# Attention and two gated layers on one core: where the first scores, the sums, the filler units, X's copies and the column loads stand

## The chip, the cores and the metric

One core of one Trainium2 chip. The metric is the device time of one execution in microseconds, measured on the chip. All times below come from the timed runs or from one profiled execution. The engines are named as the profile names them: PE (TensorE), ACT (ScalarE), DVE (VectorE), POOL (GpSimd), and SP (SyncE, which issues most DMAs).

## The reference, cut to what matters

The program is an attention with capped scores, then a gated layer that mixes along the sequence, then a gated convolution layer. All is float32; batch 2, 12 heads, sequence 448, head size 64, model width 768, inner width 1024.

```
scores = scale * q @ k.T;  scores = cap * tanh(scores / cap)
attn = softmax(scores);    x = attn @ v, heads side by side     # 2 x 448 x 768
h = gelu(x @ w_in);        u, v = halves of h
v_n = layer norm of v (with g_ln);  v_s = w_sg @ v_n + b_sg
y = x + (u * v_s) @ w_out
h2 = relu(y @ w2_in);      conv = three taps along the sequence (conv_w)
out = (h2 * sigmoid(conv)) @ w2_out
```

## The kernel before

Everything is computed in split form: a float32 value is kept as a high and a low part, and one product is three matmuls (`mm3`, L108 to L111).

**Attention** (`attention`, L273) works on 12 pairs of heads. A loop over half pairs R (L592) writes the program; two half pairs make a pair, N = R // 2. For a half pair, `scores` (L383) puts scores into the tile `sc` (four PSUM banks, one buffer), `soft` runs tanh on ACT from PSUM into `raw` (L394), `expo` runs exp in place (L403). In the first half pair (R = 0) the scores come in two groups of two banks, each with its own tanh and exp; all later half pairs have one tanh and one exp. The sum over the two 128-key groups, `sm`, is added on DVE (L449).

The products with v go into the tile `pv`, which is called `sums` in the code (three banks, L381): `value` (L458) multiplies the exponentials with v, the rest of `values` (L479) multiplies them with ones, which gives the softmax sums. Pairs use two overlapping ranges of the tile, so the value products of a pair wait until ACT has copied the last pair's to E (`copy`, L521). `LAGS` says by how many half pairs `values` runs behind `scores`; for the first half pair the value products come in R = 1 right behind its scores (L611).

`norm` (L505) takes two pairs of heads at a time: the sums go through DRAM to be reciprocals spread over partitions (POOL's DMAs, L523, L545, L551), DVE multiplies E with them (L558), and `split` writes the high part of X on ACT (L105) and the low part on DVE (L106). The last pair takes a way over PE (`norm_pe`, L567). Steps are put off by `later(k, fn)`, k ticks on; there are two ticks in each R.

`idle` matmuls (L440, the table `IDLE`) multiply zeros in the bank `mo`: four behind the first scores group, two behind the scores of R = 1, nine behind those of R = 3.

**Filler.** The table `FILL` puts the first four units of the next layer (18 matmuls each, `mmw`) into the attention: unit 0 in thirds at R = 15, 19 and 23, in the bank `mo`; units 1, 2 and 3 at R = 24, 25 and 26 in the banks 1 to 3 of one tile `fi`, which takes the place of `sc` (L633). `u_done` runs their gelu: a square on ACT (L221), a product on DVE (L224), a tanh on ACT (L225), a product u on DVE (L228).

**Loads.** SP issues the DMAs in the order of the program: q, k and v of coming pairs, and a piece of `w_in` at each R of `WIN`. A piece lands in one of four buffers (`f64`) and is converted by `decode_half` (L134): a head on ACT or DVE (L149, L151), three steps on DVE. `columns` (L269, called at R = 6) loads g_ln and the small conv_w and converts the latter on ACT and DVE (L149, L154, L158, L163).

**The rest** (`rest`, L712) runs on PE without a hole in before: units of u (`u_unit`) and of v (`v_unit`, L746), which take seven banks of a new pool and, every fourth, the bank `mo`, then the mix along the sequence, the out projection and the convolution layer. A scheduler orders each engine's instructions from the program's order and from its own estimate, but `ordered` (L374) keeps the attention's matmuls in the order written, and `pin` holds ACT's and DVE's marked steps behind each other.

Of the kernel before, what the change touches and what calls it, by code (L numbers as in the profile page):

```python
# [9 lines left out]
F32 = mybir.dt.float32  # L10
# [9 lines left out]
P = 128  # L20
# [12 lines left out]
LAGS = (1, 2, 3)  # L33
# [6 lines left out]

WARM = 18

IDLE = {0: (0, 4), 1: (3, 2), 3: (3, 9)}

WIN = (3, 5, 7, 9, 12, 15, 17, 19, 21, 22, 23, 24)
WOS = (0, 1, 4, 7, 7, 10, 11, 15)
# [5 lines left out]
def stages(  # L52
# [23 lines left out]
    def pin(last):  # L76
        return tc.issue_after(last[0].ins) if last[0] is not None else ExitStack()
# [11 lines left out]
    def later(k, fn):  # L89
        due.setdefault(now[0] + k, []).append(fn)  # L90
# [177 lines left out]

    def columns(pool):  # L269
        sync(gbc, g_ln.partition_broadcast(P))  # L270
        decode(cw[:, 0], cw[:, 1], conv_w, pool, 4 if bounded else 3)

    def attention(att, psa):  # L273

# [105 lines left out]
        late, sm0 = [], [None]  # L380
        sums = psa.tile([P, 3 * 512], F32, tag="pv", name="pv", bufs=1)  # L381

        def scores(N, half, ahead={}):  # L383

            R = 2 * N + half
            q, K = Qt[N], Kt[N % 2]
            ps = psa.tile([P, 4, 512], F32, tag="sc", name="sc", bufs=1)
            raw = raws[N, half] = att.tile([P, 4, S], F32, tag="raw", name="raw", bufs=3)

            sc = {"scale": qscale} if N == 0 else {}  # L390

            def soft(x, ps):
                with pin(lasta):
                    lasta[0] = A.activation(x, ps, AF.Tanh, **sc)  # L394
                if N == 1 and half:
                    with pin(lasta):
                        late.pop()()
                if half or N:
                    expo(x)

            def expo(x):
                with pin(lasta):
                    lasta[0] = A.activation(x, x, AF.Exp, scale=creg)  # L403

            if half:
                ps = ps.rearrange("p (h a) c -> p h (a c)", h=2)[:, :, : 3 * 288]
                ps = ps.rearrange("p h (i c) -> p h i c", i=3)[:, :, :, :HS]
                raw = raws[N, half] = raw[:, :3].rearrange("p t s -> p (t s)").rearrange(
                    "p (h i c) -> p h i c", h=2, i=3
                )  # L410

            for g in range(2 * half, 2 * half + 2):
                if g in ahead:
                    ahead[g]()
                c = slice(g * P, (g + 1) * P)
                if g < 3:

                    for i, (j, l) in enumerate(((0, 0), (0, 1), (1, 0))):
                        for h in range(2):
                            r = slice(h * D, (h + 1) * D)  # L420
                            out, x = ps[:, g * 2 + h, :S] if g < 2 else ps[:, h, :2], q[r, l]
                            if g == 2:
                                x = x.rearrange("p (i c) -> p i c", i=2)
                            ordered(out, lhsT=K[r, j, c], rhs=x, start=i == 0, stop=i == 2)
                else:

                    qr, _ = qraw.pop(N)
                    for h in range(2):
                        r = slice(h * D, (h + 1) * D)
                        for i in range(2):  # L430
                            ordered(
                                ps[i * D : (i + 1) * D, h, 2], lhsT=klast[N % 2][r],
                                rhs=qr[r, i * HS : (i + 1) * HS], start=True, stop=True,
                            )
                if N == 0 and g < 2:
                    soft(raw[:, 2 * g : 2 * g + 2], ps[:, 2 * g : 2 * g + 2, :S])
                    if g:
                        expo(raw[:, 0:2])
                        expo(raw[:, 2:4])
                if R in IDLE and g == IDLE[R][0]:  # L440
                    for _ in range(IDLE[R][1]):
                        ordered(idle, lhsT=wz[:, :P], rhs=wz, start=True, stop=True)
            if half:
                soft(raw, ps)
            elif N:
                soft(raw, ps[:, :, :S])
            if half == 0:
                held[N] = att.tile([P, 2, S], F32, tag="sm", name="sm", bufs=2)
                sm = V.tensor_tensor(out=held[N], in0=raw[:, 0:2], in1=raw[:, 2:4], op=ALU.add)  # L449
                if N == 0:  # L450
                    sm0[0] = sm
# [53 lines left out]
        def norm(N, both):  # L505
            b, p = divmod(N, NPAIR)
            if N >= B * NPAIR - NFAST:
                return norm_pe(N, both)

            j = N % 2  # L510
            last = N == B * NPAIR - NFAST - 1
            m = 1 if last else 2
            if j == 0:
                pairs[:] = (
                    att.tile([P, 2 * (S + HS)], F32, tag="E", name="E", bufs=3),
                    att.tile([P, 14], F32, tag="ss", name="ss", bufs=2)[:, : 7 * m],
                )
            e, ss = pairs

            def copy():  # L520
                lasta[0] = A.activation(e[:, j * (S + HS) : (j + 1) * (S + HS)], both, AF.Copy)  # L521
                u = j * (2 * S + HS)
                G.dma_start(ss[j * P // m : (j + 1) * P // m], e[::32, u : u + HS])  # L523

            if N:
                copy()
            else:
                late.append(copy)
            if j == 0 and not last:
                return  # L530

            rb = att.tile([P, 2, S], F32, tag="rb", name="rb", bufs=2)
            eb = e[:, HS : HS + m * S].rearrange("p (j c) -> p j c", j=m)
            rb = rb[:, :m]

            ds = []


            def s1():
                with pin(lastv):  # L540
                    V.tensor_scalar(out=ss, in0=ss, scalar1=guard, scalar2=None, op0=ALU.add)
                V.reciprocal(out=ss, in_=ss)
                ds.append(dr.tile([m, 2, 2, HS], F32, tag=f"d{m}", name="d"))
                d = ds[0]
                G.dma_start(d.rearrange("j h f (p c) -> (j h f p) c", c=7 * m), ss)  # L545

            def s1b():
                (d,) = ds
                for h in range(2):
                    for i in range(m):  # L550
                        G.dma_start(  # L551
                            rb[h * D : (h + 1) * D, i].rearrange("p (f c) -> p f c", f=2),
                            d[i, h].partition_broadcast(D),
                        )

            def s2():
                with pin(lastv):
                    V.tensor_tensor(out=eb, in0=eb, in1=rb, op=ALU.mult)  # L558
                with pin(lasta):
                    lastv[0] = split(eb, X[:, 0, p - j : p + 1, b], X[:, 1, p - j : p + 1, b], "a")  # L560

            k = 5 if N < 8 else 4
            later(k, s1)
            later(k + 1, s1b)
            later(14 if N < 8 else 13, s2)

        def norm_pe(N, both):  # L567

# [22 lines left out]
        done = 0  # L591
        for R in range(2 * NN + LAGS[1] + 1):  # L592
            N, half = divmod(R, 2)
            if R == 6:
                columns(att)
            if R == 4:
                load_vlast(3, NN)
# [4 lines left out]
            if R < 2 * NN:  # L602
                if half == 0 and N + 2 < NN:
                    load(N + 2)
                if half == 0 and N + 1 < NN:
                    load_v(N + 1)
                if R == 1:

                    start_values(0)
                    scores(N, half)  # L610
                    value(0, 0)  # L611
                    value(0, 1)
                    values(0, 0, True)
                    done += 1
                else:
                    scores(N, half)
                if half == 0 and N + 1 < NN:
                    with pin(sm0) if N == 1 else ExitStack():
                        prep_q(N + 1)
                        prep_k(N + 1)  # L620
            if R in FILL:

                i, k0, k1 = FILL[R]
                if k0 == 0:
                    if i == 1:
                        free = psa.tile([P, 4, 512], F32, tag="sc", name="fi", bufs=1)
                    fill[i] = free[:, i, :S] if i else psm.tile([P, 512], F32, tag="mo", name="mo")[:, :S]
                for k in range(k0, k1):
                    mmw(fill[i], 0, i, k, ordered)
                if k1 == NK:  # L630
                    u_done(0, i, fill[i])
            tick()
            if done < 2 * NN and R - done >= LAGS[R >= LAGS[2]]:  # L633
                values(*divmod(done, 2))
                done += 1
            tick()
# [414 lines left out]
```

## Time and profile before

| what | value |
|---|---|
| median of 3 runs | 333.09 us (332.92 to 335.06) |
| the profiled execution | 333.06 us |
| its span, first to last instruction | 331.3 us |
| mean granted clock of PE | 0.996 |
| busy: PE, DVE, ACT, POOL | 317.9, 239.0, 222.9, 36.9 us |

The span is shorter than the execution's time by what lies around it. A share of busy time is a mean over stages with different limits; where PE is almost always busy, its few waits and the work that computes nothing are what a change can win. In the rows below, a timeline row gives start and duration in microseconds, the engine, the line, the operation, the tile written and the tiles read, the sizes, how many such instructions follow each other, and in brackets how long the engine stood idle ahead of it and what ended that.

### The profile page before, as it was taken

How to read it: one execution, taken by the hardware profiler on the slowest of the kernel's cores; microseconds unless marked ns; L12 is line 12 of the kernel's file. 1: busy time of each engine (PE TensorE's matmuls, PEld its weight loads, DVE VectorE, ACT ScalarE, POOL GpSimd, SP SyncE). 2: the span in 40 equal slices, each digit the busy share in tenths (PEclk: the TensorE clock that was granted, in tenths of full speed). 3: DMA queues.
4: the chain of work that ended last, by engine and by line, in shares of the span. 5: the costliest groups of instructions: out<-in, count | busy, mean ns of one | idle time of the engine just before them, and what ended most of it. 6: DMA issues, size and time to landing. Idle time of an engine off the chain costs nothing.

```text
span 331.3 us, 6291 instructions
## 1 busy us (share of the span) xinstructions
PE 317.9 (96%) x2391; PEld 263.5 (80%) x2391; DVE 239.0 (72%) x470; ACT 222.9 (67%) x356; POOL 36.9 (11%) x73
## 2 busy tenths in 40 slices
PE   8899999999999989999999999999999999999992
PEld 6566666566667768988899999999999999999991
DVE  4456876487467589999998798996868999990000
ACT  3799899998993257676855565545677989883110
POOL 4000134030332211112111000000000000000000
PEclk9999999999999999999999999999999999999998
DMA  5498664745732132322403690001292123013210
GB/s 141 126 202 245 209 206 126 198 152 152 241 99 54 57 123 70 91 65 70 130 6 122 195 353 8 2 0 63 64 345 102 32 65 95 0 54 118 83 59 34
DMA packets 22063, 37.75 MB, mean 114 GB/s; under 512 B 7320, under 2 KB 14376, under 8 KB 22024
## 3 DMA queue, kind: packets, MB, share of 16 engines
q1 hardware_dynamic: 20152, 34.41, 33.1%
q0 software_dynamic: 1632, 2.61, 2.9%
q8 instruction: 21, 0.34, 0.4%
q10 hardware_dynamic: 240, 0.23, 0.3%
q14 instruction: 18, 0.15, 0.1%
HBM read 34.40 MB, written 2.79 MB: 112 GB/s over the span
## 4 chain that ended last, share of the span: by engine, by line
PE 77%; ACT 10%; DMA 5%; DVE 3%; SPq 2%; issue 1%; DVEq 0%; ACTq 0%
PE mo L109 18%; PE mo L110 18%; PE mo L111 18%; PE pv L377 6%; ACT raw L394 4%; PE fi L377 3%; PE sc L377 3%; ACT raw L403 3%; PE mo L756 3%; PE mo L757 3%; PE mo L758 3%; SPq L83 2%; DMA kr<-in_kT_dram 2%; DMA f<-in_w_in_dram 2%; DMA qr<-in_qT_dram 1%; PE mo L377 1%
## 5 line engine op out<-in xcount | busy, mean ns | idle before, releaser
L111 PE MATMUL mo<-X,WI 128*128 128x448 f32 x120 | 43.8, 365 | 0.0
L110 PE MATMUL mo<-X,WI 128*128 128x448 f32 x120 | 43.8, 365 | 0.0
L109 PE MATMUL mo<-X,WI 128*128 128x448 f32 x120 | 43.2, 366 | 0.0
L403 ACT ACTIVATE raw<-raw 128x1344 f32<-128x1344 f32 (+2 forms) x25 | 36.4, 1460 | 0.6
L377 PE MATMUL pv<-raw,V 128*32 128x224 f32 x576 | 32.9, 358 | 2.1 <-ACT E L521 2.1
L110 PE MATMUL mo<-HG,W 128*128 128x448 f32 x96 | 34.7, 365 | 0.0
L111 PE MATMUL mo<-HG,W 128*128 128x448 f32 x96 | 34.7, 365 | 0.0
L394 ACT ACTIVATE raw<-sc 128x1792 f32<-128x1792 f32 (+1 forms) x22 | 32.4, 1472 | 3.3 <-PE sc L377 3.2
L109 PE MATMUL mo<-HG,W 128*128 128x448 f32 x96 | 33.3, 365 | 0.0
L179 ACT ACTIVATE f<-f 128x256 f32<-128x256 f32 (+2 forms) x44 | 22.8, 517 | 14.9 <-DMA f<-in_w_in_dram 7.9
L377 PE MATMUL sc<-Q,K 64*128 64x448 f32 x216 | 28.8, 387 | 1.6 <-ACT raw L394 1.1
L377 PEld LDWEIGHTS pv<-raw,V 128*32 128x32 f32 x576 | 18.9, 109 | 13.7 <-issue 4.9
L377 PEld LDWEIGHTS sc<-Q,K 64*128 64x128 f32 x216 | 18.4, 184 | 11.9 <-ACT raw L394 6.5
L189 DVE SCALAR_TENSOR_TENSOR f<-f 128x256 uint32<-128x256 uint32 (+2 forms) x44 | 22.4, 518 | 6.9 <-ACT f L182 6.7
L109 PEld LDWEIGHTS mo<-X,WI 128*128 128x128 f32 x120 | 22.5, 188 | 2.2 <-ACT g L225 0.4
L111 PEld LDWEIGHTS mo<-X,WI 128*128 128x128 f32 x120 | 22.5, 188 | 1.9
L110 PEld LDWEIGHTS mo<-X,WI 128*128 128x128 f32 x120 | 22.5, 188 | 1.9
L182 ACT ACTIVATE f<-f 128x256 uint32<-128x256 uint32 (+2 forms) x44 | 22.6, 514 | 0.0
L192 DVE SCALAR_TENSOR_TENSOR f<-f 128x256 uint32<-128x256 uint32 (+2 forms) x44 | 22.5, 517 | 0.2
L936 ACT ACTIVATE o<-mo 128x448 f32<-128x448 f32 x12 | 6.3, 544 | 23.0 <-PE mo L111 19.9
L449 DVE TENSOR_TENSOR sm<-raw 128x896 f32<-128x896 f32 x12 | 13.1, 1090 | 11.0 <-ACT raw L403 10.8
L109 PEld LDWEIGHTS mo<-HG,W 128*128 128x128 f32 x96 | 18.0, 188 | 1.5
(151 smaller groups left out, 700.3 us busy)
## 6 DMA issues: line engine op xcount, KB each, us to landing
f<-in_w_in_dram SPq DMA_DIRECT2D x12, 512.0 KB, 3.9
f<-in_w_out_dram SPq DMA_DIRECT2D x24, 256.0 KB, 5.0
f<-in_w_in_dram SPq DMA_DIRECT2D x12, 511.8 KB, 4.7
f<-in_w_out_dram SPq DMA_DIRECT2D x8, 384.0 KB, 3.2
qr<-in_qT_dram SPq DMA_DIRECT2D x24, 112.0 KB, 3.2
out_dram<-o SPq DMA_DIRECT2D x12, 224.0 KB, 1.9
rb<-d POOLq DMA_DIRECT2D x22, 112.0 KB, 3.5
V<-in_vL_dram SPq DMA_DIRECT2D x12, 192.0 KB, 2.6
```

What stands on the lines that cost most here:

```text
L109: matmul(ps, lhsT=whi, rhs=xhi, start=start, stop=False)
L110: matmul(ps, lhsT=whi, rhs=xlo, start=False, stop=False)
L111: matmul(ps, lhsT=wlo, rhs=xhi, start=False, stop=stop)
L179: A.activation(f(h), f(h), AF.Copy, scale=2.0**-112)
L182: A.activation(l, l, AF.Copy, scale=0.93 * 2.0**-29)
L189: V.scalar_tensor_tensor(out=l, in0=h, scalar=3, in1=l, op0=ALU.logical_shift_left, op1=ALU.bitwise_or)
L192: V.scalar_tensor_tensor(out=l, in0=h, scalar=0x80000000, in1=l, op0=ALU.bitwise_and, op1=ALU.bitwise_or)
L377: lastm[0] = T.matmul(*args, **kw)
L394: lasta[0] = A.activation(x, ps, AF.Tanh, **sc)
L403: lasta[0] = A.activation(x, x, AF.Exp, scale=creg)
L449: sm = V.tensor_tensor(out=held[N], in0=raw[:, 0:2], in1=raw[:, 2:4], op=ALU.add)
L756: T.matmul(ps, lhsT=xs(0, k), rhs=WI[1][:, 0, k], start=k == 0, stop=False)
```

## The change

Five parts, all in the attention:
1. The first scores group (R = 0, g = 0) goes into the accumulators' tile (`sums`, seen as three banks) and its tanh reads from there. `IDLE` becomes four matmuls behind the second group, none at R = 1, five at R = 3.
2. The sums of the first half pair are multiplied behind the scores of the second pair (R = 2), no longer ahead of them; `R > 1` keeps `values` from running earlier.
3. X of a pair of pairs is split in two halves: one at the old tick, one two ticks later (one tick for late pairs).
4. Filler units 2 and 3 use the one bank `mo` in turn; only unit 1 stays in a tile in the place of `sc`.
5. `columns` is called at R = 23, ahead of that R's weight piece, and its conversion steps come 5, 6 and 7 ticks behind.

```diff
-IDLE = {0: (0, 4), 1: (3, 2), 3: (3, 9)}
+IDLE = {0: (1, 4), 3: (3, 5)}
...
-        decode(cw[:, 0], cw[:, 1], conv_w, pool, 4 if bounded else 3)
+        decode(cw[:, 0], cw[:, 1], conv_w, pool, *((4, (5, 6, 7)) if bounded else (3,)))
...
-        def scores(N, half, ahead={}):
+        def scores(N, half):
...
-                if g in ahead:
-                    ahead[g]()
+                to = ps
+                if R == 0 and g == 0:
+                    to = sums.rearrange("p (t c) -> p t c", t=3)
...
-                            out, x = ps[:, g * 2 + h, :S] if g < 2 else ps[:, h, :2], q[r, l]
+                            out, x = to[:, g * 2 + h, :S] if g < 2 else ps[:, h, :2], q[r, l]
...
-                    soft(raw[:, 2 * g : 2 * g + 2], ps[:, 2 * g : 2 * g + 2, :S])
+                    soft(raw[:, 2 * g : 2 * g + 2], to[:, 2 * g : 2 * g + 2, :S])
...
                     V.tensor_tensor(out=eb, in0=eb, in1=rb, op=ALU.mult)
+                part(0)
+
+            def part(i):
                 with pin(lasta):
-                    lastv[0] = split(eb, X[:, 0, p - j : p + 1, b], X[:, 1, p - j : p + 1, b], "a")
+                    lastv[0] = split(eb[:, i], X[:, 0, p - j + i, b], X[:, 1, p - j + i, b], "a")
...
             later(14 if N < 8 else 13, s2)
+            if j:
+                later(16 if N < 8 else 14, lambda: part(1))
...
-            if R == 6:
+            if R == 23:
                 columns(att)
...
+                else:
+                    scores(N, half)
+                if R == 2:
                     values(0, 0, True)
                     done += 1
-                else:
-                    scores(N, half)
...
-                    fill[i] = free[:, i, :S] if i else psm.tile([P, 512], F32, tag="mo", name="mo")[:, :S]
+                    fill[i] = free[:, i, :S] if i == 1 else psm.tile([P, 512], F32, tag="mo", name="mo")[:, :S]
...
-            if done < 2 * NN and R - done >= LAGS[R >= LAGS[2]]:
+            if R > 1 and done < 2 * NN and R - done >= LAGS[R >= LAGS[2]]:
```

The first order shown is PE's, at the start of the program, as the difference from before to after: `wps` is warm-up, K_87 belongs to the first pair and K_88 to the second, `sm` is the summed exponentials of the first half pair.

```order
 L351 MATMUL wps<-wz 128x448 x18
+L377 MATMUL pv<-Q,K_87 128x448 x6
 L377 MATMUL sc<-Q,K_87 128x448 x6
 L377 MATMUL idle<-wz 128x448 x4
-L377 MATMUL sc<-Q,K_87 128x448 x6
 L377 MATMUL sc<-Q,K_87 128x2x224 x6
 L377 MATMUL sc<-qr,kl_91 64x224 x4
-L377 MATMUL idle<-wz 128x448 x2
 L377 MATMUL pv<-raw,V 32x224 x16
+L377 MATMUL sc<-Q,K_88 128x448 x12
 L377 MATMUL pv<-sm,ones_148 32x224 x4
-L377 MATMUL sc<-Q,K_88 128x448 x12
```

The first group now writes `pv`, the idles stand behind both groups, two idles are gone, and the second pair's twelve scores matmuls stand ahead of the four sums matmuls.

The second is PE's again, at the end of the attention, around the last filler unit: the `ones` rows end the last pair's sums, the eighteen of `fi` or `mo` are unit 3, `E,sel` is the last pair's normaliser.

```order
 L377 MATMUL pv<-raw,ones_146 32x224
 L377 MATMUL pv<-raw,ones_147 32x224
-L109 MATMUL mo<-X,WI_76 128x448
-L110 MATMUL mo<-X,WI_76 128x448
-L111 MATMUL mo<-X,WI_76 128x448
-L109 MATMUL mo<-X,WI_76 128x448
-L110 MATMUL mo<-X,WI_76 128x448
-L111 MATMUL mo<-X,WI_76 128x448
-L377 MATMUL fi<-X,WI_76 128x448 x18
+L377 MATMUL mo<-X,WI_76 128x448 x18
 L377 MATMUL pv<-E,sel 64x224 x4
```

The six matmuls of a later unit that stood ahead of unit 3 have gone from there, and unit 3 now writes the bank `mo`.

The third is ACT's, in the middle of the attention, where X is copied and a weight piece (`hd`) is converted. Before:

```order
L403 ACTIVATE raw<-raw 128x1792
L105 ACTIVATE X<-E 128x2x448
L394 ACTIVATE raw<-sc 128x1344
L403 ACTIVATE raw<-raw 128x1344
L521 ACTIVATE E<-pv 128x672
L149 ACTIVATE hd_140<-f_878 128x512
L394 ACTIVATE raw<-sc 128x1792
```

And after:

```order
L403 ACTIVATE raw<-raw 128x1792
L105 ACTIVATE X<-E 128x448
L394 ACTIVATE raw<-sc 128x1344
L403 ACTIVATE raw<-raw 128x1344
L522 ACTIVATE E<-pv 128x672
L105 ACTIVATE X<-E 128x448
L149 ACTIVATE hd_141<-f_867 128x512
L394 ACTIVATE raw<-sc 128x1792
```

The copy of two heads' X became two copies, the second behind the copy E and straight ahead of the piece's conversion and the next tanh.

## Rows read from the trace of the kernel before

**Rows 1.** The page, busy time of each engine, share of the span, instructions.

```profile
PE 317.9 (96%) x2391; PEld 263.5 (80%) x2391; DVE 239.0 (72%) x470; ACT 222.9 (67%) x356; POOL 36.9 (11%) x73
```

**Rows 2.** What PE waited for: total us, times, longest.

```profile
PE pv L377 <- ACT E L521: 2.1, 4, 0.6
PE mo L756 <- DVE u L228: 1.6, 1, 1.6
...
PE sc L377 <- ACT raw L394: 1.1, 1, 1.1
PE fi L377 <- DVE u L228: 0.5, 1, 0.5
```

**Rows 3.** Stretch, length, busy us of PE, PEld, DVE, ACT, POOL, clock, DMA, GB/s.

```profile
10.00:11.00 1.00, 0.16 (x2) 0.16 (x4) 0.00 (x0) 1.00 (x2) 0.00 (x0) 1.00 0.59 120
...
140.00:150.00 10.00, 10.00 (x48) 8.72 (x47) 10.00 (x23) 7.55 (x15) 1.00 (x1) 1.00 0.25 79
```

**Rows 4.** Timeline of the start, PE and ACT, 7.8 to 22 us.

```profile
7.80 1.01 ACT L394 ACTIVATE raw<-sc,one 128x896 f32<-128x896 f32 x1 [1.46 <-PE sc L377]
...
9.78 1.01 ACT L394 ACTIVATE raw<-sc,one 128x896 f32<-128x896 f32 x1 [0.97 <-PE sc L377]
...
10.69 1.78 ACT L403 ACTIVATE raw<-raw 128x896 f32<-128x896 f32 x2
...
10.84 0.88 PE L377 MATMUL sc<-Q,K 64*128 64x448 f32 x6 [1.10 <-ACT raw L394]
...
12.19 0.67 PE L377 MATMUL idle<-wz 128*128 128x448 f32 x2
12.37 1.37 ACT L394 ACTIVATE raw<-sc,one 128x1344 f32<-128x1344 f32 x1
...
12.79 1.76 PE L377 MATMUL pv<-raw,V 128*32 128x224 f32 x32
...
14.33 0.60 PE L377 MATMUL pv<-sm,ones 128*32 128x224 f32 x8
...
14.86 1.49 PE L377 MATMUL sc<-Q,K 64*128 64x448 f32 x12
...
16.39 1.67 ACT L394 ACTIVATE raw<-sc 128x1792 f32<-128x1792 f32 x1 [1.29 <-PE sc L377]
...
18.49 0.88 PE L377 MATMUL sc<-Q,K 64*128 64x448 f32 x6
...
19.84 2.09 PE L377 MATMUL idle<-wz 128*128 128x448 f32 x9
19.97 1.30 ACT L394 ACTIVATE raw<-sc 128x1344 f32<-128x1344 f32 x1 [0.19 <-PE sc L377]
...
21.86 1.48 PE L377 MATMUL sc<-Q,K 64*128 64x448 f32 x12
```

**Rows 5.** Timeline, around the columns' conversion, 28 to 38 us.

```profile
28.66 0.36 DVE L103 CAST K<-kr 128x384 fp32r<-128x384 f32 x1 [2.94 <-DMA kr<-in_kT_dram]
...
35.56 0.22 ACT L158 ACTIVATE cw<-f 128x24 fp32r<-128x24 f32 x1 [0.57 <-DVE f L154]
...
37.67 1.76 PE L377 MATMUL pv<-raw,V 128*32 128x224 f32 x32 [0.58 <-ACT E L521]
```

**Rows 6.** ACT's copies of X by shape: count, busy us, mean ns, idle before.

```profile
L105 ACT ACTIVATE X<-E 128x896 fp32r<-128x896 f32 x5 | 4.7, 938 | 0.6 <-DVE E L558 0.6
...
L105 ACT ACTIVATE X<-E 128x448 fp32r<-128x448 f32 x2 | 1.1, 566 | 2.1 <-DVE E L558 2.1
```

**Rows 7.** Timeline, last filler unit and first gating unit, 110 to 119 us.

```profile
110.62 0.62 DVE L228 SCALAR_TENSOR_TENSOR u<-g,fi 128x448 f32<-128x448 f32 x1 [0.65 <-ACT g L225]
...
110.88 0.47 PE L109 MATMUL mo<-X,WI 128*128 128x448 f32 x1
...
112.20 3.82 PE L377 MATMUL fi<-X,WI 128*128 128x448 f32 x18
...
118.57 0.50 PE L756 MATMUL mo<-WI,X 128*128 128x512 f32 x1 [1.64 <-DVE u L228]
```

## Prediction

> **What bounds the kernel now.** I read the page's busy shares first: TensorE (PE) is busy 96% of the span, the next engine, VectorE (DVE), 72% [rows 1]. So the reader is to look at what is left of PE's time, and that is the list of what PE waited for: 2.1 us in four waits of the value products for ScalarE's (ACT's) copy E, 1.6 us of a gating unit for DVE's u, 1.1 us of the first scores for a tanh, 0.5 us of a filler unit for u [rows 2]. All of these lie before 119 us; behind that PE waits for nobody. A gain must therefore come out of the first 119 us, and out of these waits or out of filler matmuls that count as busy but compute nothing. The latter show in the timeline as groups named "idle", of two at 12.19 and of nine at 19.84 [rows 4]; a third, of four, stands between the first two scores groups.
>
> In the loop over head pairs PE and ACT are nearly level: a pair's tanh, exp, tanh, exp and copy follow each other on ACT, PE's products follow theirs, and each waits a little for the other. So something that starts both earlier at the head keeps its gain, and every extra ACT instruction costs PE about what it lasts.
>
> **The start, step by step (times of before, then of after).** The two scores groups of the first half pair shared one tile, so the second group stood behind the first tanh. That tanh runs 7.80 to 8.81; the second tanh starts at 9.78 because its scores came only then [rows 4]. With the first group in the accumulators' tile the second follows at once, and the second tanh follows the first on ACT. ACT instructions that don't need each other overlap by 0.1 (10.69 starts 0.1 ahead of the end of 9.78 + 1.01), so it starts at 8.71, 1.07 earlier. The two exps then end at 11.40 instead of 12.47.
> - Scores of the second half wait for that second tanh: 10.84 becomes 9.77. Their two groups of matmuls hold PE 1.35 (10.84 to 12.19). Then two idle matmuls stood until 12.79; they are gone, so the value products start at 9.77 + 1.35 = 11.12. The first order shown has this; their first eight wait for the first exp only, their second eight for the second, which 0.77 later, at 11.89, is done.
> - The second pair's scores now come ahead of the sums: 11.12 + 1.54 (12.79 to 14.33) = 12.66. They need the tile that the half pair's tanh frees: 11.30 + 1.37 = 12.67. So 12.72 instead of 14.86.
> - Their tanh moves from 16.39 to 14.25 and ends at 15.92. PE pays the sums (0.53, 14.33 to 14.86) now, behind the scores, and reaches the next scores at 12.72 + 1.41 + 0.53 + 2.21 = 16.87 (1.41 is a group of twelve's share of PE, 2.21 the products up to 18.49). That is only 1.6 earlier than 18.49, and not stopped by the tanh.
> - The next tanh, 19.97, becomes 16.87 + 1.35 (18.49 to 19.84) + 0.04 = 18.26 and ends at 19.56. Before, nine idles held PE from 19.84 to 21.86 though the tanh was done at 21.27; five are through at 19.3. The third pair's scores start at 19.61 instead of 21.86.
>
> That is 2.25. From there both engines follow each other as before, and ACT, which is 2.1 early, doesn't hold PE back: I take **2.2**. Bounds: 1.1, the shift of the second tanh alone, if the reordering gave nothing, and 2.4.
>
> **Clock.** PE was busy 0.16 of the microsecond from 10 to 11, and the granted clock of that row is 1.00, the 2.4 GHz level [rows 3]. The widest hole of the changed start is shorter, about 0.6 (behind the four idles, which then end at 9.2, until 9.77), so I charge nothing for the six idles that go. The Trainium skill (TensorE: Matmul & The Clock Gate, section What's actually happening) says that the clock is gated to 1.2 GHz by default and that only recent activity releases it, so that taking filler away can cost speed; by that rule the sum would be the slower rival's below, and the trace of before does not bear it out for a hole of 1.1 us.
>
> **Columns behind the pieces.** Two ACT conversions of the columns (0.22 for the second, and ACT stood 0.57 for DVE ahead of it) delayed E, and PE stood 0.58 at 37.67 [rows 5]. They now stand at the end of attention, where ACT waits for PE anyway, and two SP issues leave the loads' queue at 26 us. Gain **0.6**, between 0.4 and 0.7. Moved, the conversions come between two filler units; there they could delay the normaliser's copy, but its reciprocal ends about when PE gets there, so 0 to 0.2 lost, counted below.
>
> **X in halves.** The other three waits for E cost (2.1 - 0.58) / 3 = 0.5 each [rows 2, 5]. Each follows one copy of two heads' X, 0.94; a half copy is 0.57 [rows 6], so the pair costs 0.2 more ACT time but half of it comes later. In the first of the three the half saves 0.37 of the 0.5. In the other two the second half stands with the conversion of a weight piece straight ahead of the next tanh (third order shown); PE has then only moved its wait from E to that tanh, and loses the 0.1 or so that the split costs each time. Sum 0.4 - 0.1 - 0.1 = **0.2**; bounds -0.3 (all three pay the split and save nothing) and 0.9 (each saves 0.3).
>
> **Units in turn in one bank.** The second filler unit shared a tile with the first and waited 0.5 for its u [rows 2]. Now unit 2 takes the bank of unit 0, which is long free: +0.5. Unit 3 must take unit 2's bank and so wait for its u, which in before ended at 110.62 + 0.62 = 111.24, with PE free at 110.88 [rows 7]. Before, PE put six matmuls of a later unit into that gap, 110.88 to 112.20; these now come later, so they are no gain, and PE stands about 0.4. Behind unit 3, the gating units took banks of the fillers' tile and stood 1.64 at 118.57; that tile is now free after unit 1, so they follow the normaliser's four matmuls: +1.6. Small loss at the normaliser 0.1. Sum 0.5 - 0.4 + 1.6 - 0.1 = **1.6**; bounds 0.3, if unit 3 or the gating units find another wait of a microsecond, and 2.1.
>
> **Behind 119 us.** Everything is pulled ahead, but DVE has no room in places: 10.00 of the 10 us from 140 to 150 [rows 3]. It can follow the 3 us of the start, since it is pulled ahead with it, less surely the 1.6 of the end. PE didn't wait there in before, so there was slack of unknown size; loss between 0 and 1.6, I take 0.2, near nothing because no wait is in the row.
>
> **Sum.** 2.2 + 0.6 + 0.2 + 1.6 - 0.2 = 4.4. The profiled execution took 333.06 (span 331.3, 1.8 around it), the median of the three runs is 333.09, so the two are one. 333.06 - 4.4 = **328.7**, span 326.9.
>
> **Rivals.**
> 1. *The loads hold the start back.* DVE stood 2.94 at 28.66 for the fourth prefetched k [rows 5], and the row sums of the pair in work stand behind that on DVE. Pulled ahead by 2.2, PE would wait for these. For: the wait is there, and SP's queue is full. Against: SP's first loads of this stretch lose a register load ahead of them, about 1 us, and the columns' two issues, and PE's need of the sums lies more than a microsecond behind. If it comes, the start keeps 1.0: gain 3.2, 329.9. Chance 0.12.
> 2. *The end gives nothing.* Unit 3's wait grows, since ACT has X halves and column conversions around it, or the gating units run into the last weight piece, whose conversion follows unit 3's tanh. For: the chain PE, ACT, DVE, ACT, DVE stands bare now. Against: on ACT the square and the tanh of unit 2 stand next to each other, and PE puts off the last piece's products behind three units' others. Gain 4.4 - 1.3 = 3.1, 330.0. Chance 0.13.
> 3. *Slower: the clock falls.* The place is 8 to 22 us, where six idles go. The price: PE runs about 9 us of matmuls from 12.79 to 21.86 [rows 4]; no row here is at the lower level, so I bound it by twice the time, +9 at most. It decides from 4.4 us of matmul work on; with 6 the time is 334.7, slower than before. For: six of fifteen idle matmuls go, and PE now follows ACT more closely. Against: the row at 10 to 11 us. Chance 0.05.
> 4. *It does less than it says.* ACT, not PE, carries the loop, and the 2.2 shrink to the shift of the second tanh, 1.1, with the X halves at -0.3: gain 2.8, 330.3. Chance 0.10.
>
> **How the numbers follow.** The forecast keeps 0.60. A change within 1% (3.3 us) is what a measurement of this kernel can hardly tell from none. The likeliest case spreads over gains of 3.4 to 5.6 (its terms will hardly all end at their better bound, which would be 6.1). Rivals 1, 2 and 4 end between 2.8 and 3.2, and could end past 3.3 with a term at its better bound; I give them a quarter of their 0.35 on the faster side. Faster: 0.60 + 0.09 = 0.69; slower 0.05; within 1%: 0.26. The range holds the likeliest case to its end (333.06 - 5.6 = 327.5, taken as 327.4) and the three middling rivals up to a gain of 2.3 (330.8).
>
> **What would show it.** Start: third pair's scores near 19.6 us, no idle group between the half pair's scores and the value products, no PE wait for a tanh near 10. Columns: no wait for E near 35. X: one 0.5 us wait for E gone, two smaller, with a wait for a tanh behind them. End: unit 2 without a wait, unit 3 with 0.4, the first gating unit near 112.7 and without a wait. I am wrong if the third pair's scores come after 20.6, if a wait for DVE's sums or for K appears near 28, if the granted clock falls under 1.00 before 25 us, or if PE shows waits behind 119.

## The result and the profile after

The changed kernel takes **328.7 us** (median of 4 runs, 328.54 to 329.17) against 333.1 before in the same comparison: ratio 0.9855, 95% interval 0.9823 to 0.9888. The profiled execution took 329.17, its span is 327.4 (331.3 before). Beside later experiments the same kernel gave 328.69, ratio 0.9835 (0.9807 to 0.9863). Some executions of a kernel are about 1% longer at a lower mean granted clock (five of the twelve of undo_columns below took 333.2 to 334.8 at 0.989 to 0.992, the other seven 330.1 to 331.5 at 0.995 to 0.998), so the experiments are read by their traces first.

The page's busy shares, and below them what PE waited for (total us, times, longest), in the changed kernel; they answer to [rows 1, 2].

```profile
PE 317.0 (97%) x2385; PEld 263.1 (80%) x2385; DVE 239.6 (73%) x475; ACT 223.4 (68%) x361; POOL 36.8 (11%) x73
```

```profile
PE sc L377 <- ACT raw L394: 1.6, 4, 0.5
PE wps L351 <- DVE wz L348: 1.4, 1, 1.4
PE pv L377 <- ACT E L522: 0.7, 3, 0.2
PE mo L377 <- DVE u L228: 0.4, 1, 0.4
```

PE is about as busy as before in microseconds, in a shorter span. The gating unit's 1.6 and the filler's 0.5 for u have become one 0.4; the four waits for E, 2.1 in all, are three of 0.23. The scores wait four times for a tanh instead of once: at 10.36 and 20.38 in the start, where one wait of 1.10 stood before, and at 74.80 and 91.02, where two of the waits for E were. The timeline of the start (start, duration), PE and ACT, answers to [rows 4]:

```profile
1.38 6.16 PE L351 MATMUL wps<-wz 128*128 128x448 f32 x18 [1.38 <-DVE wz L348]
...
8.40 1.01 ACT L394 ACTIVATE raw<-pv,one 128x896 f32<-128x896 f32 x1 [2.38 <-PE pv L377]
...
9.30 1.00 ACT L394 ACTIVATE raw<-sc,one 128x896 f32<-128x896 f32 x1
...
10.36 0.88 PE L377 MATMUL sc<-Q,K 64*128 64x448 f32 x6 [0.40 <-ACT raw L394]
...
13.39 1.50 PE L377 MATMUL sc<-Q,K 64*128 64x448 f32 x12
...
17.55 0.88 PE L377 MATMUL sc<-Q,K 64*128 64x448 f32 x6
...
20.38 1.49 PE L377 MATMUL sc<-Q,K 64*128 64x448 f32 x12 [0.21 <-ACT raw L394]
```

The second tanh now follows the first on ACT without a hole. But the first tanh itself starts at 8.40, not at 7.80: the 18 warm-up matmuls (`wps`) held PE until 7.5, in before until 6.6. What lies ahead of the first tanh is called the head below. Counted from the first tanh, the third pair's scores come after 11.98 us instead of 14.06. So I give the kernels' places (start times) below counted from the first tanh.

In the middle of the attention, PE on the second half of X, and ACT ahead of it (71.99 to 73.10):

```profile
71.99 0.57 ACT L105 ACTIVATE X<-E 128x448 fp32r<-128x448 f32 x1
72.46 0.79 ACT L149 ACTIVATE hd<-f 128x512 f16<-128x512 bf16 x1
73.10 1.64 ACT L394 ACTIVATE raw<-sc 128x1792 f32<-128x1792 f32 x1
...
74.80 0.87 PE L377 MATMUL sc<-Q,K 64*128 64x448 f32 x6 [0.51 <-ACT raw L394]
```

Half of X and a weight piece's top stand ahead of the tanh, and PE's wait moves from E to that tanh; the same at 91.02. At the end of the attention, PE's row that answers to [rows 7]:

```profile
101.92 3.94 PE L377 MATMUL mo<-X,WI 128*128 128x448 f32 x18
...
108.48 3.94 PE L377 MATMUL mo<-X,WI 128*128 128x448 f32 x18 [0.40 <-DVE u L228]
112.35 0.98 PE L377 MATMUL pv<-E,sel 128*64 128x224 f32 x8
113.26 0.50 PE L763 MATMUL mo<-WI,X 128*128 128x512 f32 x1
```

Unit 2 starts without a wait, unit 3 stands 0.40, the gating unit follows the normaliser at once. Behind 119 us PE waits for nobody, as before.

### The profile page after: what moved, and what is told of

Same layout as the page of the kernel before. It is cut to its first block, busy times and chain, and to the rows that moved or that the text cites. A ratio compares the mean times of both kernels' runs of the same rounds, so it can differ in the third digit from the quotient of the medians.

```text
span 327.4 us, 6293 instructions
## 1 busy us (share of the span) xinstructions
PE 317.0 (97%) x2385; PEld 263.1 (80%) x2385; DVE 239.6 (73%) x475; ACT 223.4 (68%) x361; POOL 36.8 (11%) x73
## 4 chain that ended last, share of the span: by engine, by line
PE 87%; ACT 10%; issue 1%; DVE 1%; ACTq 0%
PE mo L109 18%; PE mo L110 18%; PE mo L111 18%; PE pv L377 10%; PE sc L377 7%; ACT raw L394 5%; PE mo L377 4%; PE mo L763 3%; PE mo L765 3%; PE mo L764 3%; ACT raw L403 2%; PE wps L351 2%; PE fi L377 1%; ACT E L522 1%; ACT X L105 1%; ACT hd L149 1%
## 5 line engine op out<-in xcount | busy, mean ns | idle before, releaser
L377 PE MATMUL sc<-Q,K 64*128 64x448 f32 x210 | 27.6, 385 | 1.6 <-ACT raw L394 1.6
```

Source lines behind the costliest of these rows:

```text
L377: lastm[0] = T.matmul(*args, **kw)
```

## The experiments

All places in the table are from timelines. "Third pair" and "gating unit" are the starts of the third pair's scores and of the first gating unit, less the start of the first tanh; 1.3 is taken off the latter where six matmuls of a later unit stand ahead of it (before, short_idle, undo_bank). The ratio is to the kernel before in the same comparison. Its median there was 333.71 beside the four undo runs, 333.92 beside tile_alone, order_alone, no_idle and warm_14, 333.88 beside short_idle and top_dve, and 334.0 beside changed_again and best. So medians of different comparisons differ by up to 0.9 us without a change of the kernel, and steps of less than that are read from the places.

| kernel | first tanh | third pair | gating unit | median us | ratio, 95% interval |
|---|---|---|---|---|---|
| before | 7.80 | 14.06 | 109.5 | 333.1 | |
| changed | 8.40 | 11.98 | 104.9 | 328.7 | 0.9855, 0.9823 to 0.9888 |
| undo_start | 7.94 | 14.06 | 106.9 | 331.07 | 0.9918, 0.9892 to 0.9943 |
| undo_columns | 8.01 | 11.97 | 106.5 | 331.39 | 0.9955, 0.9923 to 0.9986 |
| undo_halves | 8.28 | 11.96 | 105.0 | 329.45 | 0.9865, 0.984 to 0.9889 |
| undo_bank | 7.80 | 11.98 | 106.0 | 330.49 | 0.9906, 0.9876 to 0.9936 |
| tile_alone | 8.05 | 11.84 | 104.8 | 329.07 | 0.9834, 0.978 to 0.9888 |
| order_alone | 8.98 | 13.05 | 106.0 | 330.41 | 0.9866, 0.9816 to 0.9915 |
| no_idle | 8.87 | 11.95 | 104.8 | 328.84 | 0.9817, 0.9767 to 0.9867 |
| warm_14 | 7.91 | 11.96 | 104.9 | 328.64 | 0.9809, 0.976 to 0.9858 |
| short_idle | 7.89 | 12.91 | 108.6 | 333.44 | 0.9989, 0.9964 to 1.0015 |
| top_dve | 8.29 | 11.96 | 103.7 | 328.0 | 0.9827, 0.9789 to 0.9864 |
| changed_again | 7.74 | 11.96 | 104.8 | 328.69 | 0.9835, 0.9807 to 0.9863 |
| best | 7.82 | 11.84 | 102.7 | 326.37 | 0.9768, 0.974 to 0.9796 |

### Each part undone

**undo_start** (parts 1 and 2 taken back):

```diff
-IDLE = {0: (1, 4), 3: (3, 5)}
+IDLE = {0: (0, 4), 1: (3, 2), 3: (3, 9)}
...
-                if R == 0 and g == 0:
-                    to = sums.rearrange("p (t c) -> p t c", t=3)
...
+                    values(0, 0, True)
+                    done += 1
                 else:
                     scores(N, half)
-                if R == 2:
-                    values(0, 0, True)
-                    done += 1
...
```

> The changed kernel with its start as it was before: the first scores in the scores' tile again, the half pair's sums ahead of the second pair's scores, idle groups of 4, 2 and 9. Theory (the start gives about 2.1 us and the loop keeps it): 328.7 + 2.1 = 330.8 us, third pair's scores about 14.1 us behind the start of the first tanh (12.0 in the changed kernel, 14.1 before), and the waits behind 28 us as in the changed kernel. Rival (ACT carries the loop, or the loads hold it back, so the start's gain is partly lost later): 329.8 us or less, with a smaller lead at the even pairs' scores behind 28 us than at the third pair's. Of the head: if the warm-up's 18 matmuls end near 6.6 us here as in the kernel before, and not near 7.5 as in the changed one's profile, the later head belongs to the change of the start; if they end late here too, it doesn't.

The first tanh and the third pair's scores:

```profile
7.94 1.01 ACT L394 ACTIVATE raw<-sc,one 128x896 f32<-128x896 f32 x1 [1.80 <-PE sc L377]
...
22.00 1.48 PE L377 MATMUL sc<-Q,K 64*128 64x448 f32 x12
```

Measured: third pair at 14.06 again, gating unit 2.07 later than in the changed kernel, 331.07 us. The start gives its 2.1, and the loop keeps all of it; the rival (lost later) falls. Its early head would have told against the start by the rule that I set down; changed_again below shows that rule to be wrong.

**undo_columns**:

```diff
-            if R == 23:
+            if R == 6:
                 columns(att)
...
-        decode(cw[:, 0], cw[:, 1], conv_w, pool, *((4, (5, 6, 7)) if bounded else (3,)))
+        decode(cw[:, 0], cw[:, 1], conv_w, pool, 4 if bounded else 3)
```

> The changed kernel with the columns' load and conversion back among the early half pairs. Theory (0.6 to 0.7 us from the wait for E): 329.3 to 329.4 us, an idle time of PE of about 0.6 us for ACT's E near 34 to 36 us. Rival (the wait was caused by the pull of the other parts too, or ACT's time there is hidden): 328.8 us or less, with no such wait.

Measured: the gating unit 1.6 later, more than the 0.6 to 0.7 expected. Timeline of DVE, ACT and PE around the conversion, 29 to 37 us:

```profile
29.57 0.47 DVE L151 CAST hd<-f 128x512 f16<-128x512 bf16 x1 [1.43 <-DMA f<-in_w_in_dram]
...
34.19 0.17 DVE L154 SCALAR_TENSOR_TENSOR f<-f,hd 128x24 uint32<-128x24 uint32 x1
...
34.40 0.23 ACT L158 ACTIVATE cw<-f 128x24 fp32r<-128x24 f32 x1 [1.29 <-DVE f L154]
...
36.51 1.76 PE L377 MATMUL pv<-raw,V 128*32 128x224 f32 x32 [1.29 <-ACT E L522]
```

ACT stands 1.29 for a tiny step of the columns on DVE, E stands behind it on ACT, and PE 1.29 behind E; in before the same chain cost 0.57 and 0.58 [rows 5]. DVE stood 1.43 for a weight piece's DMA and had no pause from there to the columns' step. That piece lands at 29.57, 0.3 earlier than in short_idle below (29.88), while the third pair's scores stand 0.8 earlier (19.98 against 20.80). So the price of the columns grows with the start's lead: 0.58 in before, 0.83 in short_idle (about 1 us ahead), 1.29 here. Most of the rest is a wait of the normaliser, 0.2. The rival, no such wait, falls. The median is higher than the trace explains, and the profiled execution is the shortest of the twelve.

**undo_halves**:

```diff
-                part(0)
...
-                    lastv[0] = split(eb[:, i], X[:, 0, p - j + i, b], X[:, 1, p - j + i, b], "a")
+                    lastv[0] = split(eb, X[:, 0, p - j : p + 1, b], X[:, 1, p - j : p + 1, b], "a")
...
-            if j:
-                later(16 if N < 8 else 14, lambda: part(1))
```

> The changed kernel with each pair's X converted in one instruction again. Theory (0.4 - 0.1 - 0.1): 328.9 us; three waits of PE for E of about 0.5 us each between 50 and 90 us, and no wait for a tanh at about 75 and 91. Rival A (the halves gain at all three places): 329.4 us or more. Rival B (the halves only cost): 328.5 us or less.

PE's waits for E in all:

```profile
PE pv L377 <- ACT E L522: 1.5, 3, 0.5
```

Measured: three waits for E of 0.49 each, none for a tanh there, and the gating unit 0.17 later; 329.45 us, 0.1 to 0.3% more than the changed kernel by the ratios. The theory of 0.2 holds in the trace; the time alone can tell it neither from rival A nor from nothing.

**undo_bank**:

```diff
-                    fill[i] = free[:, i, :S] if i == 1 else psm.tile([P, 512], F32, tag="mo", name="mo")[:, :S]
+                    fill[i] = free[:, i, :S] if i else psm.tile([P, 512], F32, tag="mo", name="mo")[:, :S]
```

> The changed kernel with units 2 and 3 back in the fillers' shared tile. Theory (1.6 to 1.7 us from the end of attention): 330.4 us; PE waits about 0.5 us for u ahead of unit 2 near 102 and about 1.6 us ahead of the first gating unit near 115. Rival (behind 119 us DVE is full, so what the end gives is lost there): 329.2 us or less, though the first gating unit is just as late.

PE at the end of the attention:

```profile
101.68 0.47 PE L109 MATMUL mo<-X,WI 128*128 128x448 f32 x1 [0.30 <-ACT X L105]
101.99 3.84 PE L377 MATMUL fi<-X,WI 128*128 128x448 f32 x18
...
115.09 0.50 PE L763 MATMUL mo<-WI,X 128*128 128x512 f32 x1 [1.25 <-DVE u L228]
```

The gating unit's wait is back, with 1.25, and 0.30 ahead of unit 2: 1.55 against the changed kernel's 0.40, so 1.1 (gating unit 106.0 against 104.9). That is less than the 1.6 to 1.7 expected and than the 1.7 that separate before and after there: in this kernel the scheduler spreads the six later matmuls one by three by two over the gaps, where before put all six into one. The median, 330.49, is the expected 330.4, but the ratios' intervals reach 1 us to either side, so the time can't tell 1.1 from 1.6. From the first gating unit to the last instruction both kernels take 214.1 to 214.2 us (with the six matmuls added in undo_bank): behind it nothing is lost, and the rival falls.

### What in the start gave the 2.1

**tile_alone**:

```diff
                     value(0, 1)
+                    values(0, 0, True)
+                    done += 1
                 else:
                     scores(N, half)
-                if R == 2:
-                    values(0, 0, True)
-                    done += 1
...
```

> The changed kernel with the half pair's sums ahead of the second pair's scores again; the first scores stay in the accumulators' tile and the idle groups are the changed kernel's 4 and 5. Theory (the shift of the second tanh alone gives 1.1 of the start's 2.1 us): 329.7 us, third pair's scores about 13.0 us behind the first tanh's start. Rival (the sums fit in while PE waits for a tanh anyway, so the order gives nothing): 328.8 us, third pair's scores at 12.0 to 12.2.

The first tanh and the third pair's scores:

```profile
8.05 1.01 ACT L394 ACTIVATE raw<-pv,one 128x896 f32<-128x896 f32 x1 [1.88 <-PE pv L377]
...
19.89 1.49 PE L377 MATMUL sc<-Q,K 64*128 64x448 f32 x12 [0.20 <-ACT raw L394]
```

**order_alone**:

```diff
-                if R == 0 and g == 0:
-                    to = sums.rearrange("p (t c) -> p t c", t=3)
...
-IDLE = {0: (1, 4), 3: (3, 5)}
+IDLE = {0: (0, 4), 3: (3, 5)}
```

> The changed kernel with the first scores back in the scores' tile; the second pair's scores stay ahead of the first's sums; idle groups of 4 and 5. Theory (what the tile gives, 1.1 us, is lost, what the order and the shorter idle groups give, about 1.0, is kept): 329.8 us, third pair's scores about 13.0 us behind the first tanh's start. Rival (the order needs the tile, since ACT has no room for it without): 330.8 us, third pair's scores at 14 us.

The same two:

```profile
8.98 1.01 ACT L394 ACTIVATE raw<-sc,one 128x896 f32<-128x896 f32 x1 [2.60 <-PE sc L377]
...
22.03 1.49 PE L377 MATMUL sc<-Q,K 64*128 64x448 f32 x12 [0.19 <-ACT raw L394]
```

**short_idle**, from the kernel before:

```diff
-IDLE = {0: (0, 4), 1: (3, 2), 3: (3, 9)}
+IDLE = {0: (0, 4), 3: (3, 5)}
```

> The kernel before, with the changed kernel's counts of idle matmuls (four behind the first scores, none behind the second half's, five in place of nine) and nothing else. Theory (about half of the start's 2.1 us comes from the idle matmuls that no longer hold PE, the rest from the tile): 1.0 us less than before in the same comparison, third pair's scores about 13.0 us behind the first tanh's start (14.06 before, 13.05 with the order and these idles, 11.84 with the tile and these idles). Rival (the idles only fill waits, and what the run of the order alone gained is the order's): within 0.3 us of before, third pair's scores at 13.8 or later.

The first tanh in short_idle, and PE at the third pair's scores and at the columns:

```profile
7.89 1.01 ACT L394 ACTIVATE raw<-sc,one 128x896 f32<-128x896 f32 x1 [1.60 <-PE sc L377]
...
20.80 1.50 PE L377 MATMUL sc<-Q,K 64*128 64x448 f32 x12 [0.19 <-ACT raw L394]
...
36.89 1.76 PE L377 MATMUL pv<-raw,V 128*32 128x224 f32 x32 [0.83 <-ACT E L521]
```

The third pair's scores give a clean sum. Fewer idles alone: 14.06 to 12.91, 1.15. The order on top of that: 13.05, 0.14 worse. The tile on top of the fewer idles: 11.84, another 1.07. All three: 11.98. So the tile (with the four idles moved behind the second group) and the fewer idles gave 1.1 each and the order nothing. Of tile_alone the theory, 13.0, falls, and the rival's reason stands. Of order_alone the theory has the place, 13.05, but it took the order and the idles together, and the whole is the idles' doing. In time, short_idle is within its interval of no change, which also holds the 1.0 us expected, so only the places tell its theory from its rival: of the 1.15 the columns took 0.25 back (0.83 against 0.58).

### The clock and the head

**no_idle** (first edit) and **warm_14** (second):

```diff
-IDLE = {0: (1, 4), 3: (3, 5)}
+IDLE = {}
...
-WARM = 18
+WARM = 14
```

> The changed kernel without the nine idle matmuls left. Theory (the clock doesn't fall for holes of a microsecond or so, and the idles only fill waits): 328.5 to 328.8 us, granted clock 1.00 in every microsecond from 8 to 25, matmuls as long as in the changed kernel. Rival (the clock rule: less activity, the lower level comes back): matmuls about twice as long somewhere between 9 and 25 us, 331 us or more.

> The changed kernel with 14 warm-up matmuls in place of 18. Theory (in the profiled execution the warm-up, most of it at about 0.36 us a matmul, held the first scores until 7.48 us though Q was ready at 6.76): the first scores come at 6.8, 0.6 to 0.7 earlier, and the time is 328.1 us. Rival (the early matmuls are what brings the clock up; with fewer the short matmuls come no sooner and the first scores themselves run slowly): 328.7 us or more, with the first two groups of scores longer than 0.9 us each.

PE's row in no_idle behind the hole, and the stretches around its two holes (busy us of PE, PEld, DVE, ACT, POOL, then the granted clock):

```profile
10.83 0.88 PE L377 MATMUL sc<-Q,K 64*128 64x448 f32 x6 [1.39 <-ACT raw L394]
```

```profile
10.00:11.00 1.00, 0.17 (x2) 0.17 (x4) 0.00 (x0) 1.00 (x2) 0.00 (x0) 1.00 0.46 138
20.00:21.00 1.00, 0.17 (x2) 0.18 (x4) 1.00 (x3) 1.00 (x2) 0.00 (x0) 1.00 0.93 233
```

Without any idle matmul PE stands 1.39 and 1.41 us, the clock stays at 1.00, the 2.4 GHz level, and the six scores matmuls behind the hole take 0.88 as in the changed kernel. The nine idles left are worth nothing here: the third pair's scores come at 11.95. In warm_14 the first scores start at 6.26, but after two matmuls PE stands 0.47 until 7.19, behind DVE's half of Q, so the first tanh starts at 7.91. Neither text has that: the early scores gained nothing, and no scores ran slowly. Its 328.64 can't be told from no_idle's 328.84 beside it.

**changed_again** is the changed kernel once more:

> The changed kernel itself once more, beside the next one on the same chip, as its measure and as one more draw of the head. If the later first tanh of its first profile (8.40 us) belongs to the change, it is late again, at 8.3 or later, though a kernel with the start undone had it at 7.94; if the moment at which the warm-up's matmuls turn short is a draw of each execution, the first tanh may stand anywhere from 7.8 to 9.0 us, and first tanh to first gating unit is 104.9 us all the same.

```profile
7.74 1.01 ACT L394 ACTIVATE raw<-pv,one 128x896 f32<-128x896 f32 x1 [1.44 <-PE pv L377]
```

Its first tanh stands at 7.74. So the 8.40 of the first profile was a draw (a difference from execution to execution), and the late head belongs to no part of the change; in the twelve profiles with 18 warm-up matmuls the first tanh stands from 7.74 to 8.98.

### A faster version

**top_dve** tests the cause of the two waits for a tanh:

```diff
-                    top_eng = "v" if R < 11 else "a"
+                    top_eng = "v" if R < 11 or R in (15, 19) else "a"
```

> The changed kernel with the first step (the top halves) of two weight pieces on DVE instead of ACT: those that stand behind the second half of X near 72 and 88 us, 0.79 us each on ACT. Theory (PE's two waits of 0.51 us for a tanh near 75 and 91 are caused by these, standing ahead of that tanh with half of X): both waits are gone, and the first gating unit comes 103.8 us behind the first tanh's start instead of 104.86, 1.0 us less in time. Rival (ACT is full anyway, the next wait for E or a tanh takes their place, or DVE, which now does 0.47 us more ahead of X's lower half and the row sums, is late): 0.4 us or less.

What PE waited for in top_dve:

```profile
PE pv L377 <- ACT E L522: 0.7, 3, 0.2
PE sc L377 <- ACT raw L394: 0.6, 2, 0.4
PE mo L377 <- DVE u L228: 0.4, 1, 0.4
```

Two of the four waits for a tanh are gone, those at 74.80 and 91.02, and the gating unit comes 1.16 earlier; the theory holds in the trace. In time it is 0.3 to 0.9 us by the ratios, less than their intervals. **best** has this edit and that of tile_alone (not shown again), and adds the first half of X on DVE and 14 warm-up matmuls:

```diff
-WARM = 18
+WARM = 14
...
-                    lastv[0] = split(eb[:, i], X[:, 0, p - j + i, b], X[:, 1, p - j + i, b], "a")
+                    lastv[0] = split(eb[:, i], X[:, 0, p - j + i, b], X[:, 1, p - j + i, b], "av"[j - i])
```

> The changed kernel with the two top halves on DVE, the first half of each pair's X converted on DVE too (0.57 us less on ACT ahead of E, three times), the half pair's sums back ahead of the second pair's scores (0.1 us), and 14 warm-up matmuls. Theory: besides the two waits of 0.51 us the three of 0.23 us for E are gone, first tanh to first gating unit 103.0 us instead of 104.9, and the time is 1.9 us or a little more under the changed kernel's beside it. Rival (ACT is so full that PE meets another wait in place of those for E, or DVE, with 1.4 us more around each pair, holds the row sums): 1.2 us or less under it, as with the top halves alone.

```profile
PE sc L377 <- ACT raw L394: 0.6, 2, 0.4
PE mo L377 <- DVE u L228: 0.4, 1, 0.4
PE pv L377 <- DVE one L368: 0.3, 1, 0.3
```

PE's waits in best: none for E is left (the 0.3 is at the first scores, which now come early). The gating unit comes at 102.7, 2.2 earlier than in the changed kernel, and the time is 326.37, 2.3 under the 328.69 beside it; the slowest of its five executions, 326.97, is faster than the fastest of the changed kernel's, 328.06. The rival, 1.2 or less, falls. Its parts were not all run alone: the waits that went and the order make 1.8 of the 2.2.

## Why the prediction was right

The forecast was 328.7. Its terms are checked below in places counted from the first tanh, and by the lead, which is a place of before less the same place of the changed kernel. The rows for the lead, first from before (the even pairs' scores and filler unit 1), then the same from the changed kernel:

```profile
35.61 1.48 PE L377 MATMUL sc<-Q,K 64*128 64x448 f32 x12
...
43.14 1.48 PE L377 MATMUL sc<-Q,K 64*128 64x448 f32 x12
...
66.03 1.48 PE L377 MATMUL sc<-Q,K 64*128 64x448 f32 x12
...
82.18 1.48 PE L377 MATMUL sc<-Q,K 64*128 64x448 f32 x12
...
98.30 3.95 PE L377 MATMUL fi<-X,WI 128*128 128x448 f32 x18
```

```profile
34.14 1.48 PE L377 MATMUL sc<-Q,K 64*128 64x448 f32 x12
...
41.01 1.48 PE L377 MATMUL sc<-Q,K 64*128 64x448 f32 x12
...
63.54 1.50 PE L377 MATMUL sc<-Q,K 64*128 64x448 f32 x12
...
79.76 1.49 PE L377 MATMUL sc<-Q,K 64*128 64x448 f32 x12
...
96.00 3.92 PE L377 MATMUL fi<-X,WI 128*128 128x448 f32 x18
```

- **The start, 2.2 forecast, 2.08 measured.** The chain came step by step: next scores 9.07 forecast, 9.15 measured; tanh 10.46 and 10.63; third pair 11.81 and 11.98. Of the last 0.17, 0.09 is a slip of the sum: in before that tanh (19.97) starts 0.13 behind the end of its scores' share of PE (19.84), and the sum has 0.04. What was wrong is the reading of the chain. The step "The second pair's scores now come ahead of the sums" was given a share, and the lower bound, 1.1, was to hold "if the reordering gave nothing". It gave nothing (tile_alone is 0.14 ahead), and 2.1 came all the same: sums and scores are the same work on PE in either order. The other half was the idles. The opening names them as a place for a gain and the steps counted them (two at 12.19, four of nine at 19.84), but the bounds give them no share. One of its signs failed too: it wanted no wait of PE for a tanh near 10, and 0.40 stands at 10.36, in the hole of about 0.6 that its own paragraph on the clock counts.
- **Columns, 0.6 forecast, 0.66 measured** in the lead from 35 to 43 us (1.47 to 2.13). With the start changed the wait would have been 1.29, so the two terms overlap: the columns had to go if the start was to keep its lead. That isn't in the prediction.
- **X in halves, 0.4 - 0.1 - 0.1 forecast, +0.36, -0.07, -0.12 measured**, in the lead from 43 us on (2.13, 2.49, 2.42, 2.30). That the last two only moved is shown: top_dve takes the pieces' conversion away, and both waits for a tanh go. No wait for E is gone, as one was to be; all three are 0.23.
- **One bank, 1.6 forecast, 1.7 measured**: PE's waits there fall from 0.5 and 1.6 [rows 2] to 0.40. The lead is 5.31 at the first gating unit, which less 1.3 for the six matmuls is 4.0, and it was 2.30 at unit 1. Unit 3's 0.40 came as forecast. undo_bank gives only 1.1, as told there.
- **Behind 119 us, -0.2 forecast, -0.1 measured**, and no wait there. This size is not shown: from the first gating unit to the last instruction the fourteen profiles take 213.7 to 214.5 us (the six matmuls added where they ran earlier), and the changed kernel alone 214.1 and 213.7 in its two.
- **The head was not forecast.** It cost 0.6 in the profiled execution and is a draw; the terms sum to 2.08 + 0.66 + 0.17 + 1.7 - 0.1 = 4.5, less 0.6 leaves 3.9; the spans differ by 3.9.

So the places bear out the sum and four of its five sizes, while the cause named for half of the first was wrong. That the median meets the forecast to 0.1 us is luck: the head alone moves by more than 1 us from profile to profile.

Of the rivals, the loads showed nothing (DVE stood 2.68 for k at 27.77, and PE didn't wait), the end gave what it should, and undo_start finds the start's 2.1 whole at the gating unit, against the rival in which ACT shrinks it. The clock is excluded for the changed start: its granted clock reads 1.00 in every microsecond from 5 to 25, and so it does in no_idle from 8 to 25, with more idle time than the change brings.

## What to carry to other kernels

Where two engines run level, undo the parts one by one and also try them alone: a part that is worth 0.6 by itself can be worth 1.3 once another has pulled the loop ahead, where what stands behind a DMA moves along less, as the columns did here. A wait that changes its name (from E to a tanh) hasn't gone; look on the engine that releases it for what stands in its queue and can run elsewhere. Count places from the first event behind the warm-up, or the draw of the head (7.74 to 8.98 here) passes for an effect of the change.

## What the runs showed of the hardware

The warm-up's matmuls are short only from a moment that differs from execution to execution. PE and PEld in the same microsecond, on the warm-up's tile alone (busy us and count, the granted clock, DMA share, GB/s), in the first profile of the changed kernel and in changed_again:

```profile
5.00:6.00 1.00, 1.00 (x4) 0.90 (x3) 1.00 0.79 222
```

```profile
5.00:6.00 1.00, 1.00 (x7) 0.90 (x6) 1.00 0.83 233
```

Four against seven matmuls of the same program touch that microsecond, and the granted clock is 1.00, the 2.4 GHz level, in both rows. Over all 18, one matmul took 575 ns (median) in the first profile of the changed kernel and 369 in before; in both the early ones take about 575 and the late ones about 365. What sets the moment no run here shows. The Trainium skill (TensorE: Matmul & The Clock Gate, section What's actually happening) says that the clock starts at half rate, that activity releases it, and that the moment varies between runs; the durations here agree with that, the clock's row doesn't show it.
